# Segment loop of a memory-token attention kernel: one stage boundary moved, copies cut in halves, three loads on other queues

## The chip, the cores and the metric

One core of a Trainium2 chip runs the whole program. The metric is the device time of one execution in microseconds (us). Engines are named as the profile names them: PE (TensorE; PEld is its weight load), DVE (VectorE), ACT (ScalarE), POOL (GpSimd) and SP (SyncE, which only issues transfers here). A `q` behind a name is that engine's instruction queue issuing a transfer or waiting.

## The reference

Two attention layers read the same tokens (2048 of width 640) and are mixed by a gate:

```python
def _A_ref(x, mem0, Wq, Wk, Wv, Wo, seg_len):      # 32 heads of 192, 8 memory rows, segments of 32
    mem = mem0
    for s in range(n_seg):                         # 64 segments, one after the other
        xs = x[:, s * seg_len:(s + 1) * seg_len, :].copy()
        h = jnp.concatenate([mem, xs], axis=1)     # 40 rows
        q, k, v = (jnp.einsum('btd,dhe->bhte', h, W) for W in (Wq, Wk, Wv))
        scores = jnp.einsum('bhqe,bhke->bhqk', q, k) * scale
        p = _softmax(jnp.where(mask, scores, -1e9), axis=-1)
        o = jnp.einsum('bhqk,bhke->bhqe', p, v)
        o = jnp.einsum('bhte,hed->btd', o, Wo)
        mem = o[:, :M, :].copy()                   # the next segment needs it
        outs.append(o[:, M:, :])
    return jnp.concatenate(outs, axis=1)

g = _sigmoid((x * gate_w).sum(-1, keepdims=True))
return g * _A_ref(...) + (1 - g) * _B_ref(...)     # B: a dilated sliding window of 8, 32 heads of 20
```

(The three projections are three lines of the reference; here they are drawn together.) Layer A is a recurrence: segment s+1 needs the memory rows that segment s put out.

## The kernel before, in words

Layer B (`part_b`) and a pass over rows that don't depend on the recurrence (`prepass`) come first and fill about the first 410 us. Then `part_a` walks the 64 segments. The program text of one segment is `segment`, in two parts, "head" (the projections Q and K of the first two thirds of the heads) and "rest" (the last third, scores, softmax, V, values, output projection). The first segment and the last "rest" stand outside a loop; `For_i` (L1030) runs 62 times and has in its body "rest" of one segment and "head" of the next.

**Work of a segment.** All tokens of a segment (24 rows of its own and 8 of memory) are the stationary operand: four weight loads of 32 columns each (`hT`, tile aH) share the array and four matmuls of 512 columns run beside each other. `m_qk(i, kcs)` projects: i = 0, 2, 4 is Q and 1, 3, 5 is K of a third of the heads, kc is a fifth of the input rows. `c_qk(i)` copies the result out of PSUM on ACT (L733 to L737), `t_qk(i)` transposes it on DVE (L743 for Q, L746 for K). `m_v(t)` and `c_v(t)` do the same for V. `scores(h)`, `e_exp(h)` (exponential on ACT, mask on DVE), `e_sum(h)` (a matmul with ones, L801) and `e_norm(h)` are the softmax of half the heads; `pv_half(h)` multiplies it with V (L847) and with the V rows of the memory tokens of all segments' last rows, which the first pass has stored and `load_vz` brings in (tile aVz, L853). `o_group` is the output projection; `pick` takes the new memory rows into `hT`.

**Weights.** What does not fit in SBUF is streamed in each segment: 21 pieces (`STREAM`) of 256 or 192 KB through seven slots (tiles wst). `release` frees a slot where its last matmul is recorded, and `pump` then issues the next piece on SP's queue; between `held()` and the next `stage()` nothing is pumped.

**Other transfers of a segment.** `load_seg` (L654, the next segment's tokens into `xh`, part of tile aK), `load_z` (L657) and `load_a4` (L667, what layer B put out for these rows, tile aG) are issued on SP's queue behind `e_exp(1)`. `load_vz` (L661) and two `store_z` (L664) are on POOL's queue. `store` (L685) is on ACT's queue. The tokens are copied from `xh` into `hT` by DVE (L1008), and `mix` (L676) reads aG in the next head.

**Order and stages.** Every engine's order is the order of the text (a manual schedule). The loop resets its semaphores without a barrier: its body has four stages, and `tc.stage_boundary()` (in `stage`) marks where one begins. An engine's first instruction behind a boundary waits until all engines have finished the stage before the previous one; `done(engines)` marks where an engine waits for its own work of the previous stage and says so to the others. In the kernel before, stage 0 is the start of "rest"; stage 1 begins at `stage(POOL)` between `m_v(1, (0,))` and `e_sum(0)`; stage 2 behind the first four `o_group`; stage 3 in the "head". SP's `done` for the previous stage stands in `held()`, and there it waits until the pieces it issued in that stage have landed.

**Where half-results stand.** `st` and `st5` (L642, L643) name the SBUF places that take the copies before the transposes: Q's last third, i = 4, is copied whole into `Px[0]`, and of K's last third the second half into `Px[0][:, 0:256]`, so that one waits for the transpose of the other. V's second third goes into `Px[1]`, which `scores(1)` still reads.

Of the kernel before, what the change touches and what calls it, by code (L numbers as in the profile page):

```python
# [12 lines left out]
I32 = mybir.dt.int32  # L13
# [14 lines left out]
class _K:  # L28
# [578 lines left out]
    def part_a(self):  # L607
        nc, tc, KC, S = self.nc, self.tc, self.KC, self.S
# [3 lines left out]
        with ctx:  # L612
            PP, KW, vz, sel, h_, a4 = self.work
            p0 = (128, 896, 1664)
            P = [PP[:, f:f + 640].rearrange("p (b c i) -> p b c i", b=5, i=8) for f in p0]
            Px = [PP[:, f + 128:f + 640] for f in p0]
            KT = KW[:].rearrange("p (c k) -> p c k", k=32)
# [4 lines left out]
            xh = KW[:, 224:384]  # L622
# [16 lines left out]
                        f = 32 * ((c1 - c0) * (j % 2) + c - c0)  # L639
                        return x[:, f:f + 32]  # L640

            st = [Px[2], Px[1], KW[:, 512:1024], Px[2], Px[0]]  # L642
            st5 = (P[1][:, 1:5, 0:8, :].rearrange("p b c i -> p b (c i)"), Px[0][:, 0:256])  # L643

            psm = ctx.enter_context(tc.tile_pool(name="psm", bufs=1, space=bass.MemoryType.PSUM))
            Ms = [psm.tile([128, 512], F32, name=f"psm{i}") for i in range(2)]
# [3 lines left out]
            def row(t, s):  # L650
                return t[bass.ds(s, 1)].rearrange("o p f -> p (o f)")

            def load_seg(s):
                nc.sync.dma_start(xh, row(self.xh_dram, s))  # L654

            def load_z(s):
                nc.sync.dma_start(PP[:, 0:2304].rearrange("p (g f) -> p g f", g=3)[:, :, 0:256],  # L657
                                  row(self.zpk_dram, s)[:, 0:768].rearrange("p (g f) -> p g f", g=3))

            def load_vz(s):  # L660
                nc.gpsimd.dma_start(vz[:], row(self.zpk_dram, s)[:, 768:1152])  # L661

            def store_z(s, h):
                nc.gpsimd.dma_start(row(self.oz_dram[h], s), zst[h])  # L664

            def load_a4(s):
                nc.sync.dma_start(a4[:].bitcast(I32), self.bsc_dram[bass.ds(32 * s, 32)].rearrange("t j f -> j t f"))  # L667

            def tail():
                pa = Ss[0][:, 0, :]  # L670
# [8 lines left out]
            def store(s, last=False):  # L679
# [4 lines left out]
                else:  # L684
# [3 lines left out]
            PE, ACTE, DVE, SP, POOL = ALL = (mybir.EngineType.PE, mybir.EngineType.Activation, mybir.EngineType.DVE,  # L688
                                             mybir.EngineType.SP, mybir.EngineType.Pool)

            pqs = [Ms[i % 2] if i // 2 == 1 or i == 4 else X[:, i % 2] for i in range(6)]

            def segment(part, prev, s, nxt, looped=False):
                pSs = {}

                def stage(*engines):
                    if looped:
                        tc.stage_boundary()
                    done(*engines)
                    self.hold = False  # L700
                    self.pump()
# [5 lines left out]
                def done(*engines):  # L707
                    if looped:
                        for e in engines:
                            tc.previous_stage_wait(e)  # L710


                def burst(ms):
                    if looped and len(ms) > 1:
                        key = ms[-1].ins.name
                        for m in ms[:-1]:
                            tc.no_tile_sem_insts.add(m.ins.name)
                            tc.add_to_no_dep_group(key, m.ins)
                        tc.declare_fence(ms[-1].ins, group=key)

                def m_qk(i, kcs):
                    p, m, pq = i // 2, "qk"[i % 2], pqs[i]
                    for kc in kcs:
                        sl = self.qk_columns((m, p, kc))
                        js = (2, 3, 0, 1) if (m, p, kc, 0) in STREAM else range(4)
                        burst([nc.tensor.matmul(pq[32 * j:32 * j + 32, :], lhsT=hT[:, kc, :], rhs=sl[j],  # L726
                                                start=(kc == 0), stop=(kc == KC - 1), tile_position=(0, 32 * j),
                                                skip_group_check=True) for j in js])
                        self.release(self.parts((m, p, kc)))

                def c_qk(i, part=None):
                    if part is None:
                        nc.scalar.copy(st[i], pqs[i])  # L733
                    elif part == 0:
                        nc.scalar.copy(st5[0], pqs[i][:, 0:256].rearrange("p (b x) -> p b x", b=4))
                    else:
                        nc.scalar.copy(st5[1], pqs[i][:, 256:512])  # L737

                def t_qk(i, part=None):

                    p = i // 2
                    if i % 2 == 0:
                        nc.vector.transpose(P[p][:, 1:5, :, :].rearrange("p b c i -> p c b i"), st[i])  # L743
                    else:
                        c0, c1 = (16 * p % 32, 16 * p % 32 + 16) if part is None else (8 * part, 8 * part + 8)
                        nc.vector.transpose(KT[:, c0:c1, :].rearrange("p c k -> p (c k)"),  # L746
                                            st[i] if part is None else st5[part])

                def cols(h):

# [32 lines left out]
                def e_exp(h):  # L783
                    E = Es[h]
                    nc.scalar.activation(E, pSs[h][:, :, 0:112], ACT.Exp, scale=scale_a)  # L785
                    nc.vector.tensor_tensor(out=E, in0=E, in1=self.mask[h].unsqueeze(1).to_broadcast([128, 2, 112]),  # L786
                                            op=ALU.mult)
# [18 lines left out]
                def e_norm(h):  # L806
                    E = Es[h]
                    rz = pSs[h][:, 0, 0:160].rearrange("p (a r q) -> p a r q", a=2, r=2)
                    nc.scalar.activation(rz, rz, ACT.Ln)
                    nc.scalar.activation(rz, rz, ACT.Exp, scale=-1.0)  # L810
                    EA, EB = (E[:, :, x] for x in cols(h))
                    EB = EB.rearrange("p a (r q) -> p a r q", r=2)
                    nc.vector.tensor_tensor(out=EA, in0=EA, in1=rz.rearrange("p a r q -> p a (r q)"), op=ALU.mult)
                    nc.vector.tensor_tensor(out=EB, in0=EB, in1=rz[:, :, :, 0:16], op=ALU.mult)

                pvs = {}

                def m_v(t, kcs=range(KC)):
                    if t not in pvs:
                        pvs[t] = Ms[1 - t % 2]  # L820
                    for kc in kcs:
                        sl = self.v_columns(t, kc)
                        burst([nc.tensor.matmul(pvs[t][32 * j:32 * j + 32, :], lhsT=hT[:, kc, :],  # L823
                                                rhs=sl[j], start=(kc == 0), stop=(kc == KC - 1),
                                                tile_position=(0, 32 * j), skip_group_check=True)
                               for j in range(4)])
                        self.release(self.parts(("v", t, kc)))

                def c_v(t):

                    (nc.vector.tensor_copy if t == 0 else nc.scalar.copy)(Px[t], pvs[t][:])  # L831

                def pv_half(h):
                    E = Es[h]
# [102 lines left out]
                self.hold = False  # L937
                self.pump()
                if prev is not None:
                    load_vz(s)  # L940
                    store(prev)
                m_qk(4, range(KC))
                done(PE, ACTE, DVE)
                m_qk(5, (0, 1, 2))
                scores(0)
                m_qk(5, (3, 4))
                if prev is None:
                    self.load_late(2)
                e_exp(0)
                c_qk(4); t_qk(4)  # L950
                c_qk(5, 0); t_qk(5, 0)
                c_qk(5, 1); t_qk(5, 1)
                m_v(0, (0, 1, 2))
# [1 line left out]
                m_v(0, (3, 4))  # L955
                c_v(0)
                m_v(1, (0,))
                stage(POOL)
                e_sum(0)
                e_norm(0)  # L960
                done(ACTE, DVE)
                m_v(1, (1, 2, 3, 4))
                done(PE)
                scores(1)
                c_v(1)
                e_exp(1)
                if nxt is None:
                    self.oz, self.oz_keys = {}, {}
                    self.oz_free = [k for p in range(3) for m in "qk" for k in self.res_tiles if k[:2] == (m, p) and len(k) == 3]
                    self.oz_free += [k for k in self.res_tiles if k[0] == "v" and len(k) == 3]  # L970
                    self.b4_free = [k for k in self.res_tiles if k[0] in "vqk" and len(k) == 4]
                    self.load_oz(0)
                if nxt is not None:
                    load_seg(nxt)
                    load_z(nxt)
                    load_a4(s)
                m_v(2, (0, 1))
                pairs = pv_half(0)
                e_sum(1)
                c_o(0, pairs)  # L980
# [17 lines left out]
                c_z(1, pairs, 0); c_z(1, pairs, 1)  # L998
                done(ACTE)
                store_z(s, 1)  # L1000
                if nxt is None:
                    self.sort_oz(0)
                for i2 in (4, 5):
                    o_group("oa", i2)
# [17 lines left out]
            ctx.enter_context(tc.manual_schedule(engines=set(ALL)))  # L1022
            self.start_stream()
            load_z(0)
            load_vz(0)
            segment("head", None, 0, 1)
            segment("rest", None, 0, 1)
            self.sent -= len(STREAM)
# [126 lines left out]
```

## Time and profile before

| | |
|---|---|
| time, median of 3 runs (lowest to highest) | 1654.86 us (1649.49 to 1656.54) |
| the profiled execution | 1656.64 us, of it span 1655.1 us |
| busy share of the span: PE, PEld, DVE, ACT, POOL | 91%, 52%, 49%, 40%, 9% |
| granted TensorE clock, mean | 0.985 |
| bytes read from and written to HBM | 402.83 MB and 39.48 MB, 267 GB/s over the span |
| SP's queue, share of 16 DMA engines | 74.4% over the span |
| time of a segment (L1008 first at 517.4, last at 1488.4, 55 of them) | 971.0 / 54 = 17.98 us |

Busy time is the union of an engine's instructions. A matmul's end is modelled, so PE at 91% is not PE at its peak. The profile splits the span into 40 slices; from slice 12 on they are the segment loop, all alike. The view of waits gives, for each waiting instruction, the total of its idle time, how often, and the longest.

### The profile page before, as it was taken

To read this page: it belongs to the slowest core of one execution; us is meant where nothing else is said; L and a number is where in the kernel's file an instruction comes from. 1 tells how busy PE (TensorE), PEld (TensorE's weight loads), DVE (VectorE), ACT (ScalarE), POOL (GpSimd) and SP (SyncE) were. 2 spreads that over 40 slices of the span, in tenths; PEclk is the share of its full clock that TensorE was granted. 3 is DMA by queue.
4 is the path that set the end of the run, shared out by engine and by line. 5 is a ranking of instruction groups with operands and counts; after the bars stand their busy time and mean duration, and the time that the engine had idled before them with its cause. 6 is when DMAs were issued, how large, how long until landed. Compare 5 with 4: busy or idle time off the path is not lost. (4 is left out here: it accounts for less than half of the span.)

```text
span 1655.1 us, 91554 instructions
## 1 busy us (share of the span) xinstructions
PE 1502.6 (91%) x37462; PEld 855.2 (52%) x37477; DVE 805.5 (49%) x2009; ACT 665.9 (40%) x1607; POOL 143.3 (9%) x275
## 2 busy tenths in 40 slices
PE   6888899798689999999999999999999999999968
PEld 3445554343345555555555555555555555555547
DVE  4656543222345555555555555555555555555520
ACT  3765642211234434344344434434434444443340
POOL 4002000010001000000100100000000010010000
PEclk9999999999799999999999999999999999999989
DMA  6941049989899999999999999999999999999981
GB/s 159 212 117 54 30 119 262 245 201 277 258 293 301 312 311 313 318 321 307 300 314 317 308 318 325 305 319 321 310 303 317 316 306 320 319 303 312 313 208 28
DMA packets 438731, 438.32 MB, mean 265 GB/s; under 512 B 194173, under 2 KB 306821, under 8 KB 438661
## 3 DMA queue, kind: packets, MB, share of 16 engines
q1 hardware_dynamic: 344344, 395.02, 74.4%
q10 hardware_dynamic: 87148, 29.72, 7.4%
q0 software_dynamic: 7168, 12.60, 2.1%
q8 instruction: 51, 0.84, 0.2%
q14 instruction: 20, 0.16, 0.0%
HBM read 402.83 MB, written 39.48 MB: 267 GB/s over the span
## 5 line engine op out<-in xcount | busy, mean ns | idle before, releaser
L726 PEld LDWEIGHTS <-aH 128*32 128x32 bf16 x7680 | 206.1, 96 | 231.2 <-issue 45.7
L823 PE MATMUL psm<-wlate_v,aH 128*32 128x512 bf16 x3200 | 253.6, 381 | 3.4 <-DVE aP L831 2.7
L733 ACT CAST aP<-psx 128x512 bf16<-128x512 f32 x128 | 68.8, 589 | 346.7 <-PE psx L726 336.0
L726 PE MATMUL psx<-wlate_k,aH 128*32 128x512 bf16 x1920 | 200.5, 384 | 0.0
L886 PEld LDWEIGHTS <-aP 128*32 128x32 bf16 x6144 | 162.9, 96 | 64.5 <-ACT aP L865 18.4
L886 PE MATMUL psm<-wlate_oa,aP 128*32 128x384 bf16 x2560 | 168.0, 329 | 0.0
L746 DVE STREAM_TRANSPOSE aK<-aP 128x512 bf16<-128x512 bf16 (+1 forms) x256 | 142.6, 557 | 15.9 <-ACT aP L733 3.2
L726 PE MATMUL psx<-wst,aH 128*32 128x512 bf16 x768 | 138.6, 383 | 3.8 <-DMA wst<-wscr 3.4
L886 PE MATMUL psm<-wst,aP 128*32 128x384 bf16 (+1 forms) x896 | 129.1, 307 | 9.5 <-DMA wst<-wscr 9.5
L743 DVE STREAM_TRANSPOSE aP<-aP 128x512 bf16<-128x512 bf16 x128 | 91.1, 712 | 95.0 <-ACT aP L733 94.8
L726 PE MATMUL psm<-wlate_q,aH 128*32 128x512 bf16 x1408 | 112.1, 384 | 18.3 <-PE psm L726 6.3
L823 PEld LDWEIGHTS <-aH 128*32 128x32 bf16 x3840 | 93.4, 97 | 67.9 <-issue 5.6
L886 PE MATMUL psm<-wlate_ob,aP 128*32 128x256 bf16 x2688 | 126.3, 274 | 2.0 <-issue 2.0
L823 PE MATMUL psm<-wst,aH 128*32 128x512 bf16 x640 | 124.7, 381 | 0.9 <-issue 0.9
L786 DVE TENSOR_TENSOR aK<-aK,aSel 128x224 bf16<-128x224 bf16 x128 | 35.3, 275 | 159.3 <-ACT aK L785 159.3
L726 PE MATMUL psx<-wres_q,aH 128*32 128x512 bf16 x1152 | 102.6, 384 | 6.6 <-DVE ZV L76 2.1
L865 DVE CAST aP<-psx 128x128 bf16<-128x128 f32 (+2 forms) x192 | 75.5, 421 | 65.1 <-PE psx L853 65.1
L726 PE MATMUL psm<-wst,aH 128*32 128x512 bf16 x512 | 100.0, 381 | 2.5 <-DMA wst<-wscr 2.1
L785 ACT ACTIVATE aK<-psS 128x224 bf16<-128x224 f32 x128 | 46.1, 360 | 134.0 <-PE psS L777 134.0
L865 ACT CAST aP<-psS 128x384 bf16<-128x384 f32 (+2 forms) x192 | 65.3, 375 | 79.3 <-PE psx L853 78.3
L831 ACT CAST aP<-psm 128x512 bf16<-128x512 f32 x128 | 75.4, 589 | 48.9 <-PE psS L777 40.4
L726 PE MATMUL psm<-wlate_k,aH 128*32 128x512 bf16 x1024 | 85.0, 379 | 0.0
(169 smaller groups left out, 2745.1 us busy)
## 6 DMA issues: line engine op xcount, KB each, us to landing
wst<-wscr SPq DMA_DIRECT2D x965, 256.0 KB, 4.6
wst<-wscr SPq DMA_DIRECT2D x384, 192.0 KB, 3.6
aP<-zpk_dram SPq DMA_DIRECT2D x64, 192.0 KB, 3.2
zpk_dram<-ZS ACTq DMA_DIRECT2D x5, 2048.0 KB
aVz<-zpk_dram POOLq DMA_DIRECT2D x64, 96.0 KB, 4.0
wlate_k<-in_A_Wk_dram SPq DMA_DIRECT2D x8, 512.0 KB
wres_q<-in_A_Wq_dram SPq DMA_DIRECT2D x7, 512.0 KB
wst<-in_A_Wk_dram SPq DMA_DIRECT2D x14, 256.0 KB
```

Source lines behind the costliest of these rows:

```text
L726: burst([nc.tensor.matmul(pq[32 * j:32 * j + 32, :], lhsT=hT[:, kc, :], rhs=sl[j], start=(kc == 0), stop=(kc == KC - 1), tile_position=(0, ...
L733: nc.scalar.copy(st[i], pqs[i])
L743: nc.vector.transpose(P[p][:, 1:5, :, :].rearrange("p b c i -> p c b i"), st[i])
L746: nc.vector.transpose(KT[:, c0:c1, :].rearrange("p c k -> p (c k)"), st[i] if part is None else st5[part])
L785: nc.scalar.activation(E, pSs[h][:, :, 0:112], ACT.Exp, scale=scale_a)
L786: nc.vector.tensor_tensor(out=E, in0=E, in1=self.mask[h].unsqueeze(1).to_broadcast([128, 2, 112]), op=ALU.mult)
L823: burst([nc.tensor.matmul(pvs[t][32 * j:32 * j + 32, :], lhsT=hT[:, kc, :], rhs=sl[j], start=(kc == 0), stop=(kc == KC - 1), tile_position ...
L831: (nc.vector.tensor_copy if t == 0 else nc.scalar.copy)(Px[t], pvs[t][:])
L865: (nc.scalar.copy, nc.vector.tensor_copy)[g](x.rearrange("p (j c q) -> p j c q", j=2, q=32), pairs[g][:, :, 0:240].rearrange("p j (c q) -> ...
L886: ms.append(nc.tensor.matmul(pso[part][32 * jj:32 * jj + 32, 0:n], lhsT=oT_slot(R // 2, j, 3 * (R % 2) + t), rhs=self.o_weights(osl, part, ...
```

## The change

The first edit is in the order of "rest": the boundary of stage 1 goes from ahead of `e_sum(0)` to behind all of `m_v(1)`, ahead of `scores(1)`; `done(ACTE, DVE)` goes behind `scores(1)` and `done(PE)` behind `m_v(2, (0, 1))`. The second: Q's last third is copied and transposed in two halves, the first ahead of `m_qk(5)` and `scores(0)` in the text, into a place inside aVz; `load_vz` therefore goes behind that transpose (and its call ahead of the first segment falls away), and the two halves of K get a place of their own. The third: the copy of V's second third is two copies with `e_exp(1)` between them. The fourth: `load_seg` goes to POOL's queue, `load_a4` to ACT's queue and to the end of the values, and `load_z` behind the first two matmul groups of `m_v(2)`. PE's instructions and their order are the same; only what they wait for differs.

```diff
-            st = [Px[2], Px[1], KW[:, 512:1024], Px[2], Px[0]]
-            st5 = (P[1][:, 1:5, 0:8, :].rearrange("p b c i -> p b (c i)"), Px[0][:, 0:256])
+            st = [Px[2], Px[1], KW[:, 512:1024], Px[2]]
+            st4 = vz[:, 0:256], Px[0][:, 0:256]
+            st5 = (P[1][:, 1:5, 0:8, :].rearrange("p b c i -> p b (c i)"), Px[0][:, 256:512])
...
             def load_seg(s):
-                nc.sync.dma_start(xh, row(self.xh_dram, s))
+                nc.gpsimd.dma_start(xh, row(self.xh_dram, s))
...
             def load_a4(s):
-                nc.sync.dma_start(a4[:].bitcast(I32), self.bsc_dram[bass.ds(32 * s, 32)].rearrange("t j f -> j t f"))
+                nc.scalar.dma_start(a4[:].bitcast(I32), self.bsc_dram[bass.ds(32 * s, 32)].rearrange("t j f -> j t f"))
...
-                def c_v(t):
+                def c_v(t, half=None):
 
-                    (nc.vector.tensor_copy if t == 0 else nc.scalar.copy)(Px[t], pvs[t][:])
+                    cs = slice(0, 512) if half is None else slice(256 * half, 256 * half + 256)
+                    (nc.vector.tensor_copy if t == 0 else nc.scalar.copy)(Px[t][:, cs], pvs[t][:, cs])
...
                 if prev is not None:
-                    load_vz(s)
                     store(prev)
                 m_qk(4, range(KC))
                 done(PE, ACTE, DVE)
+                c_qk(4, 0); t_qk(4, 0)
+                load_vz(s)
                 m_qk(5, (0, 1, 2))
                 scores(0)
                 m_qk(5, (3, 4))
...
                 e_exp(0)
-                c_qk(4); t_qk(4)
+                c_qk(4, 1); t_qk(4, 1)
                 c_qk(5, 0); t_qk(5, 0)
                 c_qk(5, 1); t_qk(5, 1)
...
                 m_v(1, (0,))
-                stage(POOL)
                 e_sum(0)
                 e_norm(0)
+                m_v(1, (1, 2, 3, 4))
+                stage(POOL)
+                scores(1)
                 done(ACTE, DVE)
-                m_v(1, (1, 2, 3, 4))
-                done(PE)
-                scores(1)
-                c_v(1)
+                c_v(1, 0)
                 e_exp(1)
+                c_v(1, 1)
...
                 if nxt is not None:
                     load_seg(nxt)
+                m_v(2, (0, 1))
+                if nxt is not None:
                     load_z(nxt)
-                    load_a4(s)
-                m_v(2, (0, 1))
+                done(PE)
                 pairs = pv_half(0)
...
                 store_z(s, 1)
-                if nxt is None:
+                if nxt is not None:
+                    load_a4(s)
+                else:
                     self.sort_oz(0)
...
             load_z(0)
-            load_vz(0)
```

`c_qk` and `t_qk` take the half as their second argument and the places from `st4` and `st5`.

More of the change, by code (lines that the diff above doesn't have):

```diff
@@ L733, in c_qk @@
                         nc.scalar.copy(st[i], pqs[i])
-                    elif part == 0:
+                    elif (i, part) == (5, 0):
                         nc.scalar.copy(st5[0], pqs[i][:, 0:256].rearrange("p (b x) -> p b x", b=4))
                     else:
-                        nc.scalar.copy(st5[1], pqs[i][:, 256:512])
+                        nc.scalar.copy((st4, st5)[i - 4][part], pqs[i][:, 256 * part:256 * part + 256])
                 def t_qk(i, part=None):
                     p = i // 2
+                    c0, c1 = (0, 16) if part is None else (8 * part, 8 * part + 8)
+                    x = st[i] if part is None else (st4, st5)[i - 4][part]
                     if i % 2 == 0:
-                        nc.vector.transpose(P[p][:, 1:5, :, :].rearrange("p b c i -> p c b i"), st[i])
+                        nc.vector.transpose(P[p][:, 1:5, c0:c1, :].rearrange("p b c i -> p c b i"), x)
                     else:
-                        c0, c1 = (16 * p % 32, 16 * p % 32 + 16) if part is None else (8 * part, 8 * part + 8)
-                        nc.vector.transpose(KT[:, c0:c1, :].rearrange("p c k -> p (c k)"),
-                                            st[i] if part is None else st5[part])
+                        c0, c1 = 16 * p % 32 + c0, 16 * p % 32 + c1
+                        nc.vector.transpose(KT[:, c0:c1, :].rearrange("p c k -> p (c k)"), x)
                 def cols(h):
```

## The prediction

> **What bounds the kernel now.** First the stretch view over the loop (columns: length, busy time of PE, PEld, DVE, ACT and POOL with counts, granted clock, busy share of the 16 DMA engines, GB/s):
>
> ```profile
> 500.00:1500.00 1000.00, 944.39 (x28194) 541.75 (x28186) 534.65 (x1442) 411.71 (x1107) 90.46 (x167) 1.00 0.94 313
> ```
>
> PE and the DMA engines are both at 94%, at full clock. A segment takes 17.98 us, so PE's idle time is about 1.0 us of it, and the transfers alone would need 0.94 x 17.98 = 16.9 us. Neither is a bound by itself: PE waits at a few places, and the transfers pause at others. The view of waits over the same stretch, and that of SP's queue, name two of them:
>
> ```profile
> PEld L801 <- issue: 38.6, 55, 1.5
> ```
> ```profile
> SPq L1030 <- DMA wst<-wscr: 62.0, 112, 1.4
> ```
>
> L801 is `e_sum(0)`, the first work of PE behind the boundary of stage 1. It waits in each of the 55 segments, 0.70 us on average, and its releaser is none that the profile can name. SP's line at L1030 (the loop's own waits) is twice a segment 0.55 us for pieces of weights to land. I put the two together: SP may not leave stage 3 until its last piece of that stage has landed, and PE may not pass the boundary before. The timeline of one segment (start, length, engine, instruction) has the rest:
>
> ```profile
> 904.59 0.55 POOL L661 DMA_DIRECT2D aVz<-zpk_dram  x1 [6.17 <-PE psm L726]
> ...
> 904.98 0.81 PE L726 MATMUL psm<-wlate_q,aH 128*32 128x512 bf16 x10
> 905.16 0.57 ACTq L685 DMA_DIRECT2D out_dram<-aG  x1
> ...
> 908.84 0.15 PEld L801 LDWEIGHTS <-aSel 128*32 128x32 bf16 x8 [0.67 <-issue]
> ...
> 911.22 0.13 PEld L853 LDWEIGHTS <-aVz 32*128 32x128 bf16 x8
> ...
> 914.90 0.19 DVE L1008 COPY aH<-aK 128x160 bf16<-128x160 bf16 x1
> ```
>
> Here `e_sum(0)` waits 0.67 us. `m_qk(4)` ends at 904.98 + 0.81 = 905.79, the V rows in aVz are first used at 911.22, the tokens at 914.90. SP's own rows behind that boundary:
>
> ```profile
> 910.71 0.34 SPq L654 DMA_DIRECT2D aK<-xh_dram  x1
> 911.26 0.40 SPq L657 DMA_DIRECT2D aP<-zpk_dram  x1
> 911.86 0.59 SPq L667 DMA_DIRECT2D aG<-bsc_dram  x1
> 912.55 15.42 SPq L467 DMA_DIRECT2D wst<-wscr  x21
> ```
>
> Three small loads stand for 912.55 - 910.71 = 1.84 us ahead of the next piece of weights, whose slot `m_v(2, (0, 1))` frees: its loads start at 910.33 in the same timeline, and its last matmuls end about 910.95. Pieces that start late are late for the next head. There 88 weight loads lie between the tail's matmuls and `scores(0)` (L777); with nothing missing they take 4.80 us:
>
> ```profile
> 828.44 1.85 PEld L726 LDWEIGHTS <-aH 128*32 128x32 bf16 x39 [0.17 <-DVE aK L924]
> ...
> 833.73 0.39 PEld L777 LDWEIGHTS <-aK 128*32 128x32 bf16 x16
> ...
> 901.25 2.72 PEld L726 LDWEIGHTS <-aH 128*32 128x32 bf16 x56 [0.16 <-DVE aK L924]
> ...
> 906.05 0.37 PEld L777 LDWEIGHTS <-aK 128*32 128x32 bf16 x16
> ```
>
> 906.05 - 901.25 = 4.80 us in one segment, 833.73 - 828.44 = 5.29 in another; over all segments the same difference has a mean of 5.15. PE's order there is fixed and nothing but pieces (and the loop's turn, which both hold) can stretch it, so about 0.35 us a segment go to pieces that have not landed.
>
> **The change part by part, for one segment.**
>
> (1) The boundary. The wait of `e_sum(0)` for SP goes; its other condition, the masked exponentials, is met at 907.66 (DVE L786, 907.38 + 0.28), over a microsecond earlier. Worth between 0.23 us (idle time of the matmuls at L801: 12.6 us for DVE L746 in 25 waits, over 55 segments) and 0.70 (of the weight loads, which run ahead of the matmuls). I take 0.42, nearer to the matmuls, since they are what PE is for: in the segment shown the last group of `m_v` starts at 908.27 (two groups from 908.06, 0.21 apart) and could be followed at 908.49, but L801's matmul starts at 908.87, 0.38 late where the load idles 0.67; the mean idles 0.70. The wait moves to `scores(1)`, which now starts at 909.62 and then would at 909.2; L801 passed at 908.84, so the landing was there by then, and the wait costs nothing. Without that cover (a landing over 0.4 us later) all 0.42 are back. Behind this wait stand all matmuls of PE, as before behind L801.
>
> (2) The halves. Q's last third was one copy of 0.58 us and one transpose of 0.71; halves are 0.39 (L735) and 0.42 (L746, 128x256) each, so ACT has 0.20 and DVE 0.13 more. V's copy of 0.59 becomes about 0.78. Both engines are idle for half of a segment (411.71 and 534.65 us of 1000). The first half now runs while PE projects K, and the second half of K's copy no longer waits for Q's transpose (0.50 us idle at L737). DVE's last transpose of K ends at 909.05 by these lengths, not 909.45, which is what lets `scores(1)` start at 909.2. Taken at 0; without it (1) shrinks by 0.3. `pv_half(0)` needs only the first half of V's copy, but that copy still starts when `scores(1)` is through; 0.
>
> (3) aVz later. Its load was issued at 904.59 and now waits for copy and transpose: 905.79 + 0.05 + 0.39 + 0.05 + 0.42 + 0.1 = 906.8. ACT is free at 905.16 + 0.57 = 905.73 and DVE at 906.0, so neither adds. This load takes 4.0 us to land (median of 64), so 910.8; use would now be at 911.22 - 0.42 = 910.8. Where the head's end is later than here, or the landing takes longer than the median, it is late; I take 0.15 given back on average. Bounds: 0 (landing in 3.7 us, the shortest on POOL's queue) and 1.9 (5.8, the longest).
>
> (4) The three loads. SP's next piece is issued at about its slot's release, some 1.5 us earlier, and the one behind it moves up too. What the head loses to pieces is 0.35; I take 0.30 as gained, bounds 0 and 0.45 (with 0.1 of waits ahead of the tail). The transfers of a segment, 16.9 us of DMA time, must then fit into a segment of 17.4. The Trainium skill, DMA: Bandwidth & Descriptors, section "Issuing engines are not separate DMA queues", says that issuing from several engines saves only the issuing sequencer's time, since all run on the same 16 DMA engines. By it the 0.30 would be 0 wherever those engines are the limit; between 908.90 and 914.90 of this segment their share is 0.88 and 0.89, so the row speaks for room just there.
>
> The loads themselves: tokens on POOL wait for aVz's landing (the `done` of the stage stands ahead of them), so they are issued at 911.0 rather than 910.71 and land, by POOL's 4.0 us, at 915.0 rather than 914.26. L1008 would otherwise run at 914.6, but DVE's next work (L1013, which waits for PE until 916.1 today) is 1.2 us behind it, so there are some 0.6 us of cover; 0, bounds 0 and 1.4 (landing in 5.8). aG on ACT is issued in a stretch where ACT idles over 5 us, and its reader L676 has 1.3 us until DVE's next transpose; 0, and 0.5 if that cover is gone. `load_z` serves the next segment's `scores(0)`, 9 us away; 0.
>
> Sum: -0.42 + 0.15 - 0.30 = -0.57 us a segment, 62 times: -35 us. The profiled execution took 1656.64 us, 1.5 of it around its span of 1655.1; it becomes 1621.6. The median of the runs shown is 1.8 lower, so 1620. The rivals are counted from that median, 1655.
>
> **The rivals.**
>
> (a) Transfers land early and aVz in time: -0.42 - 0.45 = -0.87, 1655 - 54 = 1601. For it: earlier pieces leave shorter queues. Against: aVz's sum above.
>
> (b) The boundary's wait only moves to `scores(1)`: (4) alone, 1655 - 19 = 1636. For it: in slow segments the landing is late by up to 1.4 us. Against: there pieces were issued late, which (4) mends.
>
> (c) The DMA engines are the limit, as the rule cited above has it: each gain on PE returns as a later landing, and the time stays at 1655. For it: share 0.94. Against: their share falls below 0.9 in a third of a segment, and 1.0 us of room is left.
>
> (d) Slower: POOL's chain. Copy, transpose, aVz's load, its landing, the tokens' load, its landing, L1008 now stand one behind the other. It decides when a landing on POOL's queue takes over about 4.6 us. At 4.8 aVz lands at 911.6, 0.4 later than it is used today; the tokens are issued at 911.8 and land at 916.6, L1008 is through at 916.8, and L1013, itself moved to 916.5, waits 0.3 more. With 0.3 back from (4) it is +0.4 a segment, 1655 + 25 = 1680. For it: loads and stores of aVz together land in 4.5 (median), and both loads would meet a fuller queue. Against: the load by itself shows 4.0.
>
> **How the numbers follow.** Forecast 0.50, (a) 0.14, (b) 0.09, (c) 0.12, (d) 0.15. What a measurement of this kernel can tell from no change is about 0.5%, 8 us. Forecast, (a) and (b) are faster by more: 0.73; (c) is the same: 0.12; (d) slower: 0.15. The forecast's own range is 1602 to 1640, between (a) and a sum of -0.25, in which (1) is 0.35, (3) is 0.2 and (4) is 0.1. The range of 1590 to 1662 takes in (a), (b) and (c) and leaves out (d); its lower end is a segment of 16.93 us (65 / 62 = 1.05 less), where the DMA time of 16.9 us would be all of it.
>
> **What would show it.** Right: L801's idle time in the view of waits is gone and none of its size stands at L777; L853 waits for aVz by about 0.2; SP's issues of wst follow on `m_v(2)` without the gap of 1.84 us; the 88 loads take 4.8 to 5.0; a segment takes 17.4 us with a DMA share near 0.97 (16.9 / 17.4). Wrong: PE waits at L853 or DVE at L1008 for POOL's transfers by more than 0.5 us, or the DMA share rises to 1 while the segment stays at 18.0.

## The result, and the profile after

The changed kernel took 1661.83 us (median of 17 runs, 1657.17 to 1667.73), the kernel before 1654.57 (17 runs, 1649.49 to 1658.93): a ratio of 1.0046, 95% interval 1.0032 to 1.0061. It is a little slower, by 7 us, where 35 us less were forecast. The profiled execution has a span of 1664.0 us; before it was 1655.1.

The stretch view over the same thousand microseconds of the loop, after the change (columns as before: PE, PEld, DVE, ACT, POOL, granted clock, DMA share, GB/s):

```profile
500.00:1500.00 1000.00, 919.19 (x28010) 514.52 (x28004) 541.54 (x1489) 415.20 (x1210) 120.18 (x221) 1.00 0.95 310
```

PE has fallen from 944 to 919 us of 1000 at the same clock, while a segment's work for it is the same. So PE waits more, not less, and the transfers (310 GB/s against 313) do not fill the room. The view of waits over this stretch says where (columns: total us, how often, longest):

```profile
PEld L856 <- DMA aVz<-zpk_dram: 58.7, 55, 1.4
PE psS L856 <- DMA aVz<-zpk_dram: 53.2, 54, 1.3
...
DVE aG L677 <- DMA aG<-bsc_dram: 19.6, 18, 3.6
...
DVE aH L1015 <- DMA aK<-xh_dram: 11.9, 28, 1.1
```

Line numbers have moved: L856 was L853 (the V rows of the memory tokens), L803 was L801 (`e_sum`), L677 was L676 (`mix`), L1015 was L1008 (the tokens into `hT`). The line for `e_sum` behind the boundary, 38.6 us in 55 waits before, is gone altogether. In its place PE waits in each of 55 segments for aVz, 58.7 / 55 = 1.07 us. SP's own wait for pieces has become shorter, 41.0 us where it was 62.0:

```profile
SPq L1036 <- DMA wst<-wscr: 41.0, 108, 0.9
```

The timeline of one segment has the path of aVz (start, length, engine, instruction, idle time before it and its releaser):

```profile
905.15 0.37 ACT L738 CAST aVz<-psm 128x256 bf16<-128x256 f32 x1 [0.93 <-PE psx L727]
...
905.62 0.45 DVE L746 STREAM_TRANSPOSE aP<-aVz 128x256 bf16<-128x256 bf16 x1 [0.51 <-ACT aVz L738]
...
906.51 0.28 DVE L788 TENSOR_TENSOR aK<-aK,aSel 128x224 bf16<-128x224 bf16 x1 [0.44 <-ACT aK L787]
...
906.80 0.54 POOL L662 DMA_DIRECT2D aVz<-zpk_dram  x1 [8.71 <-DVE aK L788]
...
907.41 0.32 PEld L803 LDWEIGHTS <-aSel 128*32 128x32 bf16 x8
...
911.05 0.12 PEld L856 LDWEIGHTS <-aVz 32*128 32x128 bf16 x8 [1.20 <-DMA aVz<-zpk_dram]
...
911.93 0.54 POOL L655 DMA_DIRECT2D aK<-xh_dram  x1 [4.59 <-PE psm L825]
...
914.30 0.60 ACTq L668 DMA_DIRECT2D aG<-bsc_dram  x1
...
914.84 0.20 DVE L1015 COPY aH<-aK 128x160 bf16<-128x160 bf16 x1
```

`e_sum(0)` at L803 starts without a wait. The half copy and its transpose take what was forecast: 905.15 to 906.07. But POOL's transfer starts 0.73 us behind the transpose's end, not 0.1, and PE stands 1.20 us at L856 for it. The profile names the mask (L788) as what released this start, since it ended last. But in the 55 segments its end lies 0.71 to 0.86 us behind the transpose's, while the start is always 0.73 behind; the load follows the transpose.

Where a segment's time went, from the traces, as means over 59 segments in us. The first four rows are stretches of PE's order, from weight load to weight load: the head's 88 loads, up to `scores(0)`; `m_v` from its start up to `e_sum(0)`, with the wait there; from there to `scores(1)`; and from the first load of `pv_half(0)` to the first one that needs aVz. Three kernels of the experiments stand beside them.

| | before | after | e1 (aVz early) | e5 (aVz on SP) | e8 (aVz early, aG on SP) |
|---|---|---|---|---|---|
| head's 88 loads | 5.14 | 4.99 | 5.46 | 5.38 | 4.96 |
| up to `e_sum(0)` | 1.89 | 1.29 | 1.29 | 1.30 | 1.30 |
| from there to `scores(1)` | 0.78 | 0.96 | 0.97 | 1.04 | 0.97 |
| `pv_half(0)` up to aVz | 0.25 | 1.29 | 0.14 | 0.15 | 0.12 |
| whole segment | 17.99 | 18.15 | 17.41 | 17.68 | 17.25 |

The change takes 1.04 at aVz. Up to `e_sum(0)` it gives 0.60, but 0.18 of that is back by `scores(1)`: weight loads run ahead of matmuls (by 0.21 us at L803 in the segment shown), and the first matmul of `e_sum(0)` is only 0.41 earlier behind the first of `m_v` (1.30 for 1.71). The head gives 0.15, and all the rest 0.31, half of it at the head's start, ahead of the 88 loads. Together that is +0.16 a segment, 9 to 10 us over 60 of them; the spans differ by 8.9.

### The profile page after: what moved, and what is told of

The parts are those of the page before. It is cut to its first block, busy times and chain, and to the rows that moved or that the text cites. A ratio compares the mean times of both kernels' runs of the same rounds, so it can differ in the third digit from the quotient of the medians.

```text
span 1664.0 us, 91640 instructions
## 1 busy us (share of the span) xinstructions
PE 1485.7 (89%) x37477; PEld 830.7 (50%) x37477; DVE 818.3 (49%) x2073; ACT 673.8 (40%) x1735; POOL 177.8 (11%) x338
## 5 line engine op out<-in xcount | busy, mean ns | idle before, releaser
L727 PEld LDWEIGHTS <-aH 128*32 128x32 bf16 x7680 | 186.5, 96 | 221.5 <-PE psm L727 38.7
L727 PE MATMUL psx<-wlate_k,aH 128*32 128x512 bf16 x1920 | 187.7, 382 | 0.0
L749 DVE STREAM_TRANSPOSE aK<-aP 128x512 bf16<-128x512 bf16 (+1 forms) x256 | 135.1, 547 | 7.0 <-ACT aP L734 0.2
L727 PE MATMUL psm<-wlate_q,aH 128*32 128x512 bf16 x1408 | 107.9, 382 | 17.9 <-PE psm L727 5.1
L825 PEld LDWEIGHTS <-aH 128*32 128x32 bf16 x3840 | 88.3, 97 | 69.2 <-issue 4.7
L834 ACT CAST aP<-psm 128x256 bf16<-128x256 f32 (+1 forms) x192 | 86.0, 448 | 49.6 <-PE psS L779 46.7
L856 PE MATMUL psS<-aK,aVz 32*128 32x32 bf16 (+1 forms) x1024 | 51.3, 176 | 59.3 <-DMA aVz<-zpk_dram 59.2
L746 DVE STREAM_TRANSPOSE aP<-aP 128x512 bf16<-128x512 bf16 (+1 forms) x128 | 74.0, 578 | 60.7 <-ACT aP L734 60.7
L662 POOL DMA_DIRECT2D aVz<-zpk_dram x64 | 35.0, 547 | 608.5 <-DVE aP L746 279.8
L727 PE MATMUL psx<-wres_q,aH 128*32 128x512 bf16 x1152 | 92.3, 383 | 6.4 <-DVE ZV L76 2.1
```

What stands on the lines that cost most here:

```text
L746: nc.vector.transpose(P[p][:, 1:5, c0:c1, :].rearrange("p b c i -> p c b i"), x)
L834: (nc.vector.tensor_copy if t == 0 else nc.scalar.copy)(Px[t][:, cs], pvs[t][:, cs])
L856: ms.append(nc.tensor.matmul(out[:, :, t, 0:16], lhsT=Vz[t][ks, f0 - 128 * t:f1 - 128 * t], rhs=E[ks, par, EB].rearrange("p (r q) -> p r q ...
```

## The experiments

The theory was that aVz's load, late by its new place and by POOL's queue, takes back what the rest of the change gives. Its main rivals were that the DMA engines are the limit, whatever is moved, and that the boundary or the moved loads are themselves at fault. Ratios are to the kernel before, with 95% intervals.

**e1: aVz's load early again.** The first half of Q goes through a free part of `P[2]` instead of aVz, so that the load can stand where it stood before. All else is as in the changed kernel.

```diff
-            st4 = vz[:, 0:256], Px[0][:, 0:256]
+            st4 = P[2][:, 1:5, 8:16, :].rearrange("p b c i -> p b (c i)"), Px[0][:, 0:256]
...
                 if prev is not None:
+                    load_vz(s)
                     store(prev)
...
                 c_qk(4, 0); t_qk(4, 0)
-                load_vz(s)
```

> The changed kernel with one thing mended: the first half of Q's copy stands in a free part of Px[2], so that aVz's load is issued at the start of the segment as in the kernel before. Theory (the late aVz took the gain): PE's wait for aVz, 1.07 us a segment in the changed kernel, goes to 0; 0.1 to 0.3 of it comes back at the next wait (V's copy, the tokens), so the segment falls from 18.14 to about 17.2 to 17.4 us and the time to 1600 to 1616 us. Rival (the DMA engines are the limit): the wait turns into later landings of pieces, the segment stays at 17.8 to 18.1 and the time at 1645 to 1662 us.

Measured: 1623.54 us, ratio 0.9798 (0.977 to 0.9826), faster than both kernels. The wait for aVz is gone from the view of waits, and with it the loss. The gain is smaller than expected, since another wait has grown. Stretch and waits of this kernel:

```profile
500.00:1500.00 1000.00, 963.23 (x29146) 549.33 (x29140) 559.39 (x1549) 432.89 (x1260) 125.17 (x230) 1.00 0.97 323
```
```profile
DVE aG L677 <- DMA aG<-bsc_dram: 51.2, 31, 3.4
...
ACT aP L736 <- DVE aK L749: 28.0, 21, 1.6
...
PEld L779 <- DVE aK L749: 10.8, 24, 1.2
```

DVE now waits 51.2 us in all for aG, 19.6 in the changed kernel. Its transposes come later, ACT's copies wait for them (L736), PE waits for them at `scores` (L779, 10.8 us in all; 3.3 in the changed kernel), and the head's loads take 5.46 us. A piece of weights is late there too: the one for the second fifth of `m_qk(2)` lands 1.24 us behind the first of the 88 loads, where it was 0.70 in the changed kernel. Whether aG, or a DMA share of 0.97, is what holds this kernel is a question for e8.

**e2: the halves of Q alone**, with the late load they make necessary (and K's halves in places of their own, as in the changed kernel); boundary, V's copy and the three small loads as before.

```diff
+            st4 = vz[:, 0:256], Px[0][:, 0:256]
...
-                    load_vz(s)
                     store(prev)
...
+                c_qk(4, 0); t_qk(4, 0)
+                load_vz(s)
                 m_qk(5, (0, 1, 2))
...
-                c_qk(4); t_qk(4)
+                c_qk(4, 1); t_qk(4, 1)
```

> The kernel before with Q's two halves, the first through aVz, and so the late load of aVz, and nothing else of the change. Theory: the old wait of e_sum(0) hides about 0.6 us of the lateness, the rest shows: 0.3 to 0.5 us a segment slower, 1674 to 1686 us, with a wait for aVz of about 0.5 us. Rival (DMA limit): no change, 1650 to 1660 us.

Measured: 1667.44 us, ratio 1.0074 (1.005 to 1.0099). The sign is the theory's, the size between the two. Its waits:

```profile
PEld L855 <- DMA aVz<-zpk_dram: 35.7, 53, 1.3
...
PEld L803 <- issue: 27.8, 53, 1.3
```

PE arrives later at `pv_half(0)` here, since the boundary's wait (L803) still stands ahead of it, so the wait for aVz is 0.65 us and not 1.07. The part that makes the load late is by itself slower than the kernel before. The head's 88 loads take 4.87 us here, less than the 5.14 before, though none of the three small loads was moved: while PE stands for aVz the pieces go on landing; the one for the second fifth of `m_qk(2)` lands 0.64 us behind the first of the 88 loads, 1.15 before.

**e3: the boundary alone.**

```diff
                 m_v(1, (0,))
-                stage(POOL)
                 e_sum(0)
                 e_norm(0)
-                done(ACTE, DVE)
                 m_v(1, (1, 2, 3, 4))
-                done(PE)
+                stage(POOL)
                 scores(1)
+                done(ACTE, DVE)
...
                 m_v(2, (0, 1))
+                done(PE)
                 pairs = pv_half(0)
```

> The kernel before with the boundary of stage 1 moved, and nothing else. Theory: e_sum(0) no longer waits, but scores(1) meets K's last transpose, which is not earlier here, so 0.2 to 0.4 us a segment are gained: 1630 to 1643 us. Rival (DMA limit): the gain on PE returns as later pieces, 1650 to 1657 us.

Measured: 1650.72 us, ratio 0.9964 (0.9941 to 0.9988): a miss, a quarter to a half of the gain expected. The wait ahead of `e_sum(0)` is gone in full (1.89 to 1.29 us, as in the changed kernel), but two others have come up:

```profile
PEld L847 <- DVE aK L814: 45.9, 55, 1.3
...
PE psS L847 <- ACT aK L871: 24.0, 42, 1.0
...
PE psm L823 <- DVE aP L831: 14.5, 54, 0.3
```

`m_v(2, ...)` waits 0.26 us for DVE's copy of V's first third, whose PSUM it takes over (14.5 in 54 waits; 2.2 in 11 before), and `pv_half(1)`, PE's first work behind the next boundary, idles longer at L847 (45.9 against 29.8 for the first row). That boundary needs SP's `done` for the stage before, which stands in `held()` behind all three small loads. I read this as the reason; e4 and e9 test what the parts are worth with the loads moved.

**e4: the three small loads alone**, tokens to POOL, aG to ACT, `load_z` behind `m_v(2, (0, 1))`.

```diff
-                nc.sync.dma_start(xh, row(self.xh_dram, s))
+                nc.gpsimd.dma_start(xh, row(self.xh_dram, s))
...
-                nc.sync.dma_start(a4[:].bitcast(I32), self.bsc_dram[bass.ds(32 * s, 32)].rearrange("t j f -> j t f"))
+                nc.scalar.dma_start(a4[:].bitcast(I32), self.bsc_dram[bass.ds(32 * s, 32)].rearrange("t j f -> j t f"))
```

> The kernel before with the three loads moved (tokens to POOL, residual to ACT, z behind V's matmuls), and nothing else. Theory: pieces go out earlier and the head's 88 weight loads take 4.8 to 5.0 us instead of 5.15 on average: 0.15 to 0.35 us a segment, 1633 to 1646 us. Rival (DMA limit, issuing elsewhere saves only the issue): 1650 to 1658 us.

Measured: 1638.55 us, ratio 0.9899 (0.9872 to 0.9923), in time as expected. Its waits:

```profile
PEld L801 <- issue: 36.4, 55, 1.4
...
DVE aG L676 <- DMA aG<-bsc_dram: 30.4, 24, 2.2
```

The gain is not where the expectation put it. The head's loads take 5.10 us, not 4.8 to 5.0. A segment is 0.30 us shorter (17.69 for 17.99), and of that only 0.04 lies in these loads, 0.16 in the head's start ahead of them, 0.07 in the stretch up to `e_sum(0)` and 0.05 just behind `scores(0)`; the boundary's wait is still nearly whole. And aG, now issued from ACT behind `pv_half(1)`, is late here already: no wait for this transfer stands in the view of the kernel before.

**e5: aVz's load from SP.** The changed kernel with one word changed; the place in the text is the same.

```diff
             def load_vz(s):
-                nc.gpsimd.dma_start(vz[:], row(self.zpk_dram, s)[:, 768:1152])
+                nc.sync.dma_start(vz[:], row(self.zpk_dram, s)[:, 768:1152])
```

> The kernel after with one edit: aVz's load, at the same place behind its last reader, is issued on SyncE's queue instead of GpSimd's. Theory (aVz is late by GpSimd's start of about 0.7 us behind the releaser plus a landing of 4.17 us, and that is what ate the gain): SP starts within 0.1 us, so aVz is there 0.6 us earlier at least; PE's wait of 1.07 us a segment at pv_half(0) falls to 0.5 or less, over 60 segments -34 us, 1620 to 1640. Rival (the place is the fault, whichever queue issues it, because the DMA engines are full there): the wait stays at 0.9 or more, 1650 to 1665.

Measured: 1635.87 us, ratio 0.9917 (0.9888 to 0.9946). The theory holds, its rival falls. The timeline of a segment:

```profile
911.14 0.37 ACT L738 CAST aVz<-psm 128x256 bf16<-128x256 f32 x1 [0.93 <-PE psx L727]
911.61 0.45 DVE L746 STREAM_TRANSPOSE aP<-aVz 128x256 bf16<-128x256 bf16 x1 [0.51 <-ACT aVz L738]
912.21 0.34 SPq L662 DMA_DIRECT2D aVz<-zpk_dram  x1
...
915.75 0.13 PEld L856 LDWEIGHTS <-aVz 32*128 32x128 bf16 x8
```

The issue follows the transpose by 0.15 us, ahead of the mask, and L856 does not wait. Of the 1.14 us gained at aVz a segment keeps 0.47, since the 88 loads are 0.39 longer than in the changed kernel and the head's start ahead of them 0.31. Over the segments between 500 and 1500 us, from the transpose's end to the landing: 0.73 + 4.15 = 4.88 us on POOL's queue, 0.15 + 2.92 = 3.07 us on SP's. The list of DMA issues has the landing's medians, in the changed kernel and in e5:

```profile
aVz<-zpk_dram POOLq DMA_DIRECT2D x64, 96.0 KB, 4.1
```
```profile
aVz<-zpk_dram SPq DMA_DIRECT2D x64, 96.0 KB, 2.9
```

**e6: e1 with the tokens' load on SP's queue** (the one line of e4's diff for `load_seg` turned back).

> The kernel of the early aVz (1623.54) with the tokens' load put back on SyncE's queue. If the weight pieces' issue times still decide the head's wait, each piece of the next segment is issued some 0.3 us later or more: 1630 to 1645, the head's loads above 5.6. If the DMA engines' share of 0.97 is the bound, the queue makes no difference: 1618 to 1628.

Measured: 1624.92 us, ratio 0.9831 (0.9814 to 0.9848), which overlaps e1's interval: which queue issues the tokens' load makes no difference there that can be measured. This is the time that the expectation gives for full DMA engines. It does not show them to be the reason; e8 tests that.

**e8: e1 with aG's load on SP's queue**, behind `load_z` (the expectations of e8, e10 and e11 call that the 288 KB load; the list of DMA issues has 192 KB).

```diff
-                nc.scalar.dma_start(a4[:].bitcast(I32), self.bsc_dram[bass.ds(32 * s, 32)].rearrange("t j f -> j t f"))
+                nc.sync.dma_start(a4[:].bitcast(I32), self.bsc_dram[bass.ds(32 * s, 32)].rearrange("t j f -> j t f"))
...
                     load_z(nxt)
+                    load_a4(s)
                 done(PE)
...
-                if nxt is not None:
-                    load_a4(s)
-                else:
+                if nxt is None:
```

> The kernel of the early aVz (1623.54) with aG's load put on SyncE's queue again, behind the 288 KB load. Theory A (what is left there is DVE's wait for aG at the mix, which delays the transposes): the wait of some 0.8 us a segment at the mix changes, and the time goes to 1605 to 1618. Theory B (the DMA engines, at 0.97, are the bound there): segment stays at 17.4, within 0.3% of 1623.5; the head's loads stay at 5.4 or more.

Measured: 1609.95 us, ratio 0.9748 (0.9731 to 0.9766), the fastest of all. Theory A's time comes out and B falls: the DMA share stays at 0.97 and the time still drops.

```profile
500.00:1500.00 1000.00, 968.99 (x29450) 567.62 (x29449) 569.29 (x1564) 437.88 (x1276) 126.23 (x232) 1.00 0.97 326
```
```profile
DVE aG L677 <- PE psS L672: 21.0, 58, 0.6
```

`mix` now waits for PE's matmul at L672 alone, 0.36 us each, and no longer for aG. The head's loads go from 5.46 to 4.96 us. Theory A's path, DVE's late transposes, is the smaller part of that: the wait ahead of `scores(0)` is 0.14 us shorter. The larger part is the piece for the second fifth of `m_qk(2)`, which lands 0.94 us behind the first of the 88 loads and not 1.24, and PE's wait for it falls by 0.3. Why it lands earlier (aG's transfer no longer issued from ACT just ahead of it, or PE later elsewhere) no run took apart. A segment keeps 0.16 of the 0.50; the rest has gone to other stretches, 0.16 to the head's start, 0.09 behind `scores(0)` and 0.08 ahead of `pv_half(0)`.

**e9: e1 with the boundary where it was before** (e3's diff turned back, V's halves kept).

> The kernel of the early aVz (1623.54) with the boundary put back ahead of e_sum(0), where it was before. If the boundary's wait is worth in the mended kernel what it is worth by itself in the row (0.6 us a segment): 1655 to 1662. If the DMA engines bound that kernel (share 0.97), the wait only takes the place of others: 1622 to 1635, with the head's loads shorter than 5.46.

Measured: 1635.23 us, ratio 0.9899 (0.9881 to 0.9917), between the two expectations, 0.2 us above the second. `e_sum(0)` waits again:

```profile
PEld L803 <- issue: 30.5, 54, 1.2
```

With aVz early, the moved boundary is worth 0.9899 - 0.9798 = 1.0% by the ratios; by the times it is 11.7 us, 0.7%. Alone (e3) it was 0.4%. Its stretch up to `e_sum(0)` is 0.45 us longer than in e1, the whole segment 0.24.

**e10: the changed kernel with aG's load on SP's queue** (e8's diff, without e1's).

> The kernel after with aG's load alone put back on SyncE's queue, behind the 288 KB load, as in the kernel before. Theory (in the kernel after aV z is what PE waits for, and aG's lateness, 0.36 us a segment at the mix, is mostly ahead of that wait and so hidden by it): the mix no longer waits for aG, PE's wait for aVz stays at 0.9 us or more, and the time is within 0.5% of 1662: 1654 to 1669. Rival (aG's late load is itself the loss): 0.36 us x 60 or more comes back, 1640 or less.

Measured: 1663.59 us, ratio 1.0077 (1.0053 to 1.0101): no different from the changed kernel by more than the intervals allow, as the theory had it.

```profile
PEld L856 <- DMA aVz<-zpk_dram: 61.4, 55, 1.5
...
DVE aG L677 <- PE psS L672: 19.2, 55, 0.4
```

aG is in time and nothing is gained: PE waits 1.12 us for aVz instead. The same edit is worth 0.5% by the ratios (e1 to e8; 13.6 us by the times) where aVz is early and does not hide it.

**e11: e5 with aG's load on SP's queue as well.**

> The kernel after with both aVz's load (at its new place) and aG's (behind the 288 KB load) on SyncE's queue; aVz's alone gave 1635.87. Theory (with aVz in time the 0.95 us that DVE waits for aG at the mix is the next thing on the path, as in the pair with the early aVz, which gained 13.6 us): 1618 to 1628, the head's loads at 5.1 or less from 5.38. Rival (two more issues on SyncE's queue delay the weight pieces by what aG gains): 1632 to 1640.

Measured: 1647.69 us, ratio 0.9966 (0.9944 to 0.9988): a miss, above even the rival's range, and slower than e5. The head's loads fall from 5.38 to 5.11 us as expected, but PE idles at the next boundary:

```profile
PEld L850 <- DVE aK L816: 43.3, 56, 0.9
...
PE psS L850 <- ACT aK L874: 22.6, 53, 0.5
```

In e5 the first row is 26.5 us and the second 0.6. Counted from DVE's copy of the tokens (L1014) a segment earlier, SP issues its aG load at 15.0 us and is done at 15.6; `pv_half(1)` starts at 16.0 (means over 59 segments). In e8, where aVz is not on SP's queue, the issue ends at 15.0 and `pv_half(1)` starts at 15.7 without that wait. I read this as the boundary of stage 2 waiting for SP's `done` behind aG's load, as in e3; no run took it apart further.

## Why the prediction was wrong

**Term (3), aVz's load: this is the step that failed.** The mechanism was named, the size was not found: +0.15 us a segment forecast, +1.04 measured. The prediction's chain from the end of `m_qk(4)` to the landing was 0.05 + 0.39 + 0.05 + 0.42 + 0.1 + 4.0 = 5.01 us, the very moment of use. The use was forecast well: without its wait PE would be at L856 4.99 us behind that end (a mean over 59 segments of the changed kernel, like the figures that follow). The chain was too short; it takes 6.02. POOL's start is 0.73 in place of 0.1 (+0.63), the landing 4.16 in place of 4.0 (+0.16), and the copy and the transpose start 0.19 and 0.12 behind what they wait for, in place of 0.05 each (+0.21); their own lengths add 0.01. (The profile's times on POOL are rough, so the sum of start and landing, 4.89 us in place of 4.1, is surer than its parts. The end of `m_qk(4)` is modelled.) That is 1.01 of the 1.07 us that PE waits, and more than 0.5 at that line was the prediction's own sign of being wrong. The bounds (0 to 1.9) held it; the value taken was near the low end, and its 0.1 came from no row. There were rows for it in the kernel before: two POOL stores, each behind the copy that it waits for. Timeline of the kernel before:

```profile
913.35 0.25 ACT L871 CAST aK<-psS 128x96 bf16<-128x96 f32 x1
913.98 0.54 POOL L664 DMA_DIRECT2D oz_dram<-aK  x1 [8.85 <-ACT aK L871]
...
914.74 0.25 DVE L871 CAST aVz<-psx 128x96 bf16<-128x96 f32 x1
...
915.62 0.54 POOL L664 DMA_DIRECT2D oz_dram<-aVz  x1 [1.10 <-DVE aH L1008]
```

The copies end at 913.60 and 914.99, the stores start at 913.98 and 915.62: 0.38 and 0.63 us later, not 0.1. (Behind L1008, which the row names for the second, it is 0.53.) And POOL's own load of aVz started 0.57 us behind the register move ahead of it in each of 56 segments there. With 0.6 in the sum, aVz would have been 0.5 late in the prediction's own segment, and the sum -0.07 a segment with the 0.15 for the spread kept. e5 shows this step by itself: with the start at 0.15 and the landing at 2.92 the wait is gone and the kernel is 1.3% faster (0.9917 against 1.0046).

**Term (1), the boundary:** right. -0.42 was forecast; by matmuls `e_sum(0)` is 0.41 earlier, and by weight loads `scores(1)` 0.42 (0.60 less the 0.18 that is back). Rival (b), that the wait would move to `scores(1)`, did not happen: no wait for SP of that size stands at L779. What was not foreseen is that the gain depends on term (4): alone it brings 0.4% (e3), with the loads moved and aVz early 0.7 to 1.0% (e9 to e1).

**Term (2), the halves at 0:** nothing speaks against it, though no run has the halves without either the late load or e1's other place. In e1, which has them, L856 does not wait and ACT and DVE are idle for over 40% of the stretch. Their price is the late load that comes with them, which is term (3).

**Term (4), the loads:** the size holds, the place does not. By themselves (e4) the three moves bring 0.30 a segment, as forecast, and 1.0%, 16 us, near the 19 of the prediction. But only 0.04 of it is in the 88 loads, by which the prediction priced it. The 0.15 of the changed kernel there cannot be put down to this term: e2, which has none of these moves, gives 0.27 there, while PE stands for aVz. Nor do late pieces alone stretch these loads, as the prediction has it: in e1 PE waits for DVE's transposes there too (L779). The tokens on POOL cost little, as forecast: L1015 waits 11.9 us in all, and DVE's next work still waits for PE in 50 of 55 segments. aG on ACT was put at 0 with "0.5 if that cover is gone", and the cover is gone: `mix` waits for it in 18 segments (19.6 us). In the changed kernel aVz hides that (e10); with aVz early it costs 0.5% by the ratios (e1 to e8).

**Rivals (c) and (d).** The DMA engines are not the limit of the two kernels compared: the share rose to 0.97 in e1 and e8, and the time fell. Whether they are the limit of e8 itself was not tried. The rule cited there from the Trainium skill (DMA: Bandwidth & Descriptors, section "Issuing engines are not separate DMA queues"), that another issuing engine saves only the sequencer's time, usually small, agrees with e6, where the tokens' queue made no difference. It does not agree with e5, where one load's queue was worth 1.3%. Rival (d), POOL's chain, had the right sign and the right place, but its condition (landings above 4.6 us) never came, 4.59 being the longest between 500 and 1500 us: the start was enough. Its second half, L1008 (now L1015) behind the tokens, came in part, 11.9 us in 28 segments with 1.1 the longest, and was mostly covered.

Without term (3) the prediction's own sum is -0.72 a segment, 1655 - 62 x 0.72 = 1610 us. e1, with aVz early, took 1623.54; e8, with aG in time as well, 1609.95. That e8 meets the sum is in part luck, as term (4) lies elsewhere than forecast and aG is on another queue.

## What to carry to other kernels

When a transfer is moved behind a new releaser, price it from the releaser's end to its landing, with the start read from a row of the same queue, before anything is booked as gained; a margin of zero at the point of use is a loss. Where a buffer that is loaded early is wanted for an intermediate result, look for another free place first (e1) rather than make the load late. And parts of a change are worth different amounts together than alone: a wait that hides another (aVz over aG) makes a good edit look useless, a stretch gets shorter also because PE has stood elsewhere (the head in e2), and a boundary moved without relieving the engine behind it mostly moves the wait.

## What was not expected of the hardware

POOL's DMA starts late here by a constant. In the changed kernel, between 500 and 1500 us, each of 55 loads of aVz starts 0.59 us behind the register move that its queue does ahead of it, and 0.73 to 0.74 behind the transpose's end. In e5, on SP's queue, these are 0.04 and 0.15 us, in all of 57. The landing of the same 96 KB from the same place took 4.15 us (3.23 to 4.59) on POOL's queue and 2.92 (2.45 to 3.82) on SP's. Both together make 1.8 us, from the releaser's end to the landing; this sum is surer than its parts, since the profile's times on POOL are rough.

The Trainium skill (Advanced Engine Details and Errata, section "DGE: Hardware vs Software") gives about 1 us to the first byte for GpSimd's path and about 0.6 for that of Sync and Scalar. The direction agrees; the difference measured here, 4.88 - 3.07 = 1.8 us from releaser to landing, is several times the 0.4 of those figures. How much of the longer landing is the queue's and how much is what the DMA engines carried at that moment was not tried.
